# Moving three products of the accumulating bank to later slots in a seven-product block matmul

## The chip, the cores and the metric

The kernel runs on one core of a Trainium2 chip. The metric is the device time in microseconds (us) of one execution on that core. Executions are sorted into fast and slow by their time and granted clock. "The trace" is the profile of one of them.

## The reference

The input is x, 8 batches of 3008 x 256. A discrete Fourier transform over both axes (real part) is followed by an MLP mixer: token mixing through 256 hidden units, then channel mixing through 1536 hidden units, with residual additions.

```python
def reference(x, w_tok1, w_tok2, w_ch1, w_ch2):          # cut to what matters
    x = np.fft.fft(np.fft.fft(x, axis=1), axis=2).real
    h = np.maximum(x.transpose(0, 2, 1) @ w_tok1, 0.0) @ w_tok2
    u = x + h.transpose(0, 2, 1)
    h2 = np.maximum(u @ w_ch1, 0.0) @ w_ch2               # 256 -> 1536 -> 256: the larger part
    return u + h2
```

## The kernel before

The channel part runs in 48 chunks of 512 (or 448) tokens, six per batch. A chunk has twelve *slots*. In slot `ct`, TensorE computes one block of the hidden layer (`mm1`: two matmuls of 512 columns into `pc`; a *bank* here is a buffer that matmuls write and add into), and ScalarE takes it to memory with a ReLU. The second matrix, `h @ w_ch2`, is applied to the **previous** chunk between these slots. In 41 of the chunks it is not done as eight block products but as seven (a Winograd-type scheme): the blocks are combined first, in four *sums* on VectorE, and each product is twelve matmuls of 128 columns.

```python
def sums(c1, box, k):                    # VectorE; about 0.95 us each
    a11, a12, a21, a22 = quads(c1)
    ...
    if k == 1:   tt(box[1][:], a21, a22, AT.add)          # profile: s<-c
    elif k == 2: tt(box[2][:], box[1][:], a11, AT.subtract)   # s<-s,c
    elif k == 3: tt(box[3][:], a11, a21, AT.subtract)     # s<-c
    else:        tt(box[4][:], a12, box[2][:], AT.subtract)   # s<-c,s

def mm2_seven(b, c, c1, uT, k, box):
    ...
    if k == 0:                           # pa<-wc,c: opens the accumulating bank pa
        product(box["a"], a11, wc2[:, 0:NH, 0:P], True)
    ...
    if k < 0:    tt(q[:, 0], pa, u[:, 0], AT.add)         # a bank read: q<-pa,uT
    elif k == 1:                         # pb<-wc,c: the other bank
        product(pb, a12, wc2[:, NH:NCT, 0:P], True)
        tt(lo(0), halves(pb), q[:, 0], AT.add)            # osb<-pb,q
    elif k == 2:                         # pa<-t2w,s
        product(box["a"], box[2], t2w, False)
        tt(q[:, 1], pa, u[:, 1], AT.add)                  # q<-pa,uT
    elif k == 3: product(box["b"], box[1], t1w, True)     # pb<-t1w,s
    elif k == 4:                         # pa<-t3w,s
        product(box["a"], box[3], t3w, False)
        tt(q[:, 2], pa, u[:, 3], AT.add)
        tt(hi(1), halves(box["b"]), q[:, 2], AT.add)
    elif k == 5:                         # pa<-t4w,c
        product(box["a"], a22, t4w, False)
        tt(lo(1), pa, u[:, 2], AT.add)                    # osb<-pa,uT
    elif k == 6: ...                     # pb<-b,s, the last reads, and the store
```

The texts below call a product by its `k`: the second product is k = 2, and so on; k = 0 is a chunk's first. Products 0, 2, 4 and 5 all add into one bank, `pa`. VectorE must read the partial sum between them: product 4 may not write the bank before the read after product 2 has ended, and so on.

Which slot a product and a sum get stands in two tables. The order of issue within a slot is: hidden layer, product with its bank reads, sum, *front pieces*. A front piece is a part of the Fourier transform or token mixing of the next batch, with additions of its own on VectorE (`yt`, `ut` in the profile).

```python
sum_at = {0: 1, 1: 2, 3: 4, 4: 3}                                       # slot: sum
places = {0: 0, 1: -1, 2: 1, 4: 2, 6: 3, 7: 4, 9: 5, 11: 6}             # slot: product
...
for ct in range(NCT):
    mm1(b, c, c1, ct, on_v)
    ...
        if ct in places: mm2_seven(*prev, places[ct], pbox)
        if ct in sum_at: sums(prev[2], pbox, sum_at[ct])
    ...                                        # take(nxt, 1): front pieces
    if ct == 5 and ...:                        # GpSimd folds the input of a later batch
        if joins:                              # but only once the third sum is there
            G.tensor_copy(out=hold[:], in_=pbox[3][:, 0, 0, 0:1])
        n = min(left, 6 if c == 5 or b < 2 else 5)
        take(fold2, n)
```

## Time and profile before

| | |
|---|---|
| time, median of the first 3 runs | 603.53 us (602.35 to 603.78) |
| span in the trace | 600.3 us |
| TensorE busy | 583.2 us, 97% |
| from the first product (k = 0 of the first such chunk) to the end | 532.81 us |

These are lines of the page of the kernel before: the span, the busy time of TensorE (PE), its busy tenths in 40 slices, and the granted clock in tenths.

```profile
span 600.3 us, 15332 instructions
...
PE 583.2 (97%) x6273; PEld 417.3 (70%) x6273; DVE 452.8 (75%) x924; ACT 387.3 (65%) x753; POOL 259.3 (43%) x396
...
PE   3899999999999999999999999999999999999997
...
PEclk9999999999999999999999999999999999999999
```

TensorE is at nine tenths or more in all slices but the first two and the last. The Trainium skill's page "Perfetto Trace Analysis" warns in its opening that matmul busy time is a poor measure because matmuls are pipelined; this case agrees: before the second products the page of the kernel before shows 0.5 us of idle time, where the spacing used here shows 1.43 us of stalls. What I used instead is the *spacing*: the start of a matmul minus the start of the one before it. Its common values are 56 ns for 128 columns, 189 ns for 448 and 216 ns for 512. Whatever a spacing has over the common value is a stall of TensorE, whether or not the busy row shows it. Stalls of 20 ns and more are summed in this document.

The costliest groups on the page (line, engine, operation, output and inputs | busy us, mean ns of one | idle us before them and what ended it):

```profile
L712 PEld LDWEIGHTS <-s 128*128 128x128 f16 x1968 | 122.8, 98 | 40.1 <-DVE s L90 5.7
...
L90 DVE TENSOR_TENSOR q<-pa,uT 128x256 f32<-128x256 f32 x123 | 52.3, 425 | 36.3 <-PE pa L712 35.8
...
L712 PE MATMUL pa<-t2w,s 128*128 128x128 f16 x492 | 34.2, 219 | 0.5 <-DVE s L90 0.4
L712 PE MATMUL pa<-t3w,s 128*128 128x128 f16 x492 | 34.2, 219 | 0.3 <-DVE s L90 0.2
```

Only 0.5 us of idle time is shown before the second product (0.4 of it put down to a sum), but the weight loads of the products that take sums show 5.7 us of waits on VectorE. The loads run ahead of the matmuls, so most of those 5.7 us are hidden; the spacing says how much is not.

Here is a chunk without front pieces, from the timeline of the kernel before (start us, length us, engine, line, operation, out<-in, count):

```profile
552.49 0.84 PE L712 MATMUL pa<-wc,c 128*128 128x128 f16 x12
...
552.80 0.95 DVE L90 TENSOR_TENSOR s<-c 128x1536 f16<-128x1536 f16 x1
...
553.66 0.42 DVE L90 TENSOR_TENSOR q<-pa,uT 128x256 f32<-128x256 f32 x1
...
554.00 0.95 DVE L90 TENSOR_TENSOR s<-s,c 128x1536 f16<-128x1536 f16 x1
...
555.57 0.83 PE L712 MATMUL pa<-t2w,s 128*128 128x128 f16 x12
...
556.44 0.42 DVE L90 TENSOR_TENSOR q<-pa,uT 128x256 f32<-128x256 f32 x1 [0.24 <-PE pa L712]
556.78 0.95 DVE L90 TENSOR_TENSOR s<-c 128x1536 f16<-128x1536 f16 x1
...
557.10 0.83 PE L712 MATMUL pb<-t1w,s 128*128 128x128 f16 x12
...
558.20 0.83 PE L712 MATMUL pa<-t3w,s 128*128 128x128 f16 x12
```

Read it as a chain: first sum 552.80, bank read 553.66, second sum 554.00 (it ends 554.95), second product 555.57: a margin of 0.62 us. The third sum comes at 556.78, only after the bank read that follows the second product (556.44), and ends 0.47 us before the fourth product at 558.20. With no front work there is no stall.

With front work there is. Two stalls of the kernel before, from its timeline; the bracket is the idle time before an instruction and what ended it:

```profile
228.68 0.41 DVE L90 TENSOR_TENSOR q<-pa,uT 128x256 f32<-128x256 f32 x1
...
229.01 0.94 DVE L90 TENSOR_TENSOR s<-s,c 128x1536 f16<-128x1536 f16 x1
...
230.00 0.67 PEld L712 LDWEIGHTS <-s 128*128 128x128 f16 x12 [0.53 <-DVE s L90]
230.01 0.84 PE L712 MATMUL pa<-t2w,s 128*128 128x128 f16 x12
```

```profile
88.61 0.41 DVE L90 TENSOR_TENSOR q<-pa,uT 128x256 f32<-128x256 f32 x1
...
88.94 0.95 DVE L90 TENSOR_TENSOR s<-c 128x1536 f16<-128x1536 f16 x1
...
89.94 0.67 PEld L712 LDWEIGHTS <-s 128*128 128x128 f16 x12 [0.62 <-DVE s L90]
89.94 0.84 PE L712 MATMUL pa<-t3w,s 128*128 128x128 f16 x12
```

In the first, front additions put the bank read and the second sum late; the sum ends at 229.95 and the second product starts 0.06 us later, 0.20 us after TensorE could have. In the second, the third sum, behind the bank read, ends at 89.89 and the fourth product starts 0.06 us later, 0.30 us late. In the 41 chunks the trace of before has 6 stalls before second products (1.43 us) and 3 before fourth products (0.67 us). All nine end 57 or 58 ns after the end of that product's sum.

### The profile page before, as it was taken

How to read it: one execution, taken by the hardware profiler on the slowest of the kernel's cores; microseconds unless marked ns; L12 is line 12 of the kernel's file. 1: busy time of each engine (PE TensorE's matmuls, PEld its weight loads, DVE VectorE, ACT ScalarE, POOL GpSimd, SP SyncE). 2: the span in 40 equal slices, each digit the busy share in tenths (PEclk: the TensorE clock that was granted, in tenths of full speed). 3: DMA queues.
4: the chain of work that ended last, by engine and by line, in shares of the span. 5: the costliest groups of instructions: out<-in, count | busy, mean ns of one | idle time of the engine just before them, and what ended most of it. 6: DMA issues, size and time to landing. Idle time of an engine off the chain costs nothing.

```text
span 600.3 us, 15332 instructions
## 1 busy us (share of the span) xinstructions
PE 583.2 (97%) x6273; PEld 417.3 (70%) x6273; DVE 452.8 (75%) x924; ACT 387.3 (65%) x753; POOL 259.3 (43%) x396
## 2 busy tenths in 40 slices
PE   3899999999999999999999999999999999999997
PEld 3756676677767776667767777667767777666775
DVE  8779879686898668765898678856689757866663
ACT  8854665477647866577656866568665776546662
POOL 8650555937565554527348354565555100000000
PEclk9999999999999999999999999999999999999999
DMA  8993912275138914393335942278123422233533
GB/s 160 209 178 71 177 40 55 65 141 121 37 72 127 143 37 68 79 180 54 72 60 119 129 87 54 67 145 115 37 55 84 93 55 55 64 74 76 94 72 88
DMA packets 83414, 55.69 MB, mean 93 GB/s; under 512 B 53778, under 2 KB 80082, under 8 KB 82578
## 3 DMA queue, kind: packets, MB, share of 16 engines
q1 hardware_dynamic: 76816, 36.82, 32.2%
q0 software_dynamic: 6208, 17.63, 16.3%
q8 instruction: 49, 0.80, 0.6%
q10 hardware_dynamic: 320, 0.26, 0.2%
q14 instruction: 21, 0.17, 0.1%
HBM read 35.26 MB, written 24.64 MB: 100 GB/s over the span
## 4 chain that ended last, share of the span: by engine, by line
PE 81%; DVE 1%; issue 0%; ACT 0%; DVEq 0%
PE pc L662 35%; PE pa L712 17%; PE pb L712 13%; PE pu L566 5%; PE po L775 4%; PE pt L595 3%; PE pz L471 1%; PE py L538 1%; DVE s L90 1%; PE pw L508 1%; PE pw L512 1%; DVE osb L90 0%; DVE q L90 0%; DVE ut L90 0%; ACT c L97 0%
## 5 line engine op out<-in xcount | busy, mean ns | idle before, releaser
L97 ACT ACTIVATE c<-pc 128x512 f16<-128x512 f32 (+1 forms) x553 | 312.7, 591 | 159.9 <-PE pc L662 138.8
L662 PE MATMUL pc<-ut,wc 128*128 128x512 f16 (+1 forms) x1152 | 312.4, 374 | 0.4 <-DMA wc<-in_moe_w_ch_dram 0.3
L712 PEld LDWEIGHTS <-s 128*128 128x128 f16 x1968 | 122.8, 98 | 40.1 <-DVE s L90 5.7
L662 PEld LDWEIGHTS <-wc 128*128 128x128 f16 x1152 | 98.0, 98 | 55.7 <-issue 3.0
L712 PEld LDWEIGHTS <-c 128*128 128x128 f16 x1476 | 93.1, 97 | 27.8
L90 DVE TENSOR_TENSOR s<-c 128x1536 f16<-128x1536 f16 x82 | 82.0, 1000 | 4.7 <-ACT c L97 4.7
L90 DVE TENSOR_TENSOR q<-pa,uT 128x256 f32<-128x256 f32 x123 | 52.3, 425 | 36.3 <-PE pa L712 35.8
L908 POOL COPY hold<-s 128x1 f16<-128x1 f16 x29 | 5.4, 187 | 171.5 <-DVE s L90 171.5
L90 DVE TENSOR_TENSOR osb<-pb,q 128x256 f32<-128x256 f32 x123 | 51.9, 422 | 31.1 <-PE pb L712 28.4
L90 DVE TENSOR_TENSOR ut<-pu,yt 128x512 f16<-128x512 f32 (+1 forms) x96 | 63.0, 670 | 1.6 <-PE pu L566 1.5
L90 POOL TENSOR_TENSOR eo<-sab 96x512 f16<-96x512 f16 x48 | 53.9, 1139 | 1.6
L566 PE MATMUL pu<-w2r,uu 128*128 128x512 f16 (+1 forms) x168 | 50.0, 379 | 0.0
L90 POOL TENSOR_TENSOR sab<-fa,fb 96x256 f16<-96x256 f16 (+1 forms) x72 | 46.7, 673 | 0.0
L90 DVE TENSOR_TENSOR s<-s,c 128x1536 f16<-128x1536 f16 x41 | 41.1, 1003 | 0.0
L90 DVE TENSOR_TENSOR s<-c,s 128x1536 f16<-128x1536 f16 x41 | 39.5, 964 | 0.0
L97 ACT ACTIVATE w<-pw 128x257 f16<-128x257 f32 x90 | 34.6, 384 | 6.4 <-PE pw L512 3.6
L90 DVE TENSOR_TENSOR osb<-pa,uT 128x256 f32<-128x256 f32 x41 | 17.4, 424 | 24.8 <-PE pa L712 24.7
L775 PE MATMUL po<-wc,c 128*128 128x256 f16 x288 | 35.4, 273 | 0.0
L712 PE MATMUL pa<-t2w,s 128*128 128x128 f16 x492 | 34.2, 219 | 0.5 <-DVE s L90 0.4
L712 PE MATMUL pa<-t3w,s 128*128 128x128 f16 x492 | 34.2, 219 | 0.3 <-DVE s L90 0.2
L712 PE MATMUL pb<-wc,c 128*128 128x128 f16 x492 | 34.4, 219 | 0.0
L712 PE MATMUL pa<-wc,c 128*128 128x128 f16 x492 | 34.4, 219 | 0.0
(187 smaller groups left out, 747.8 us busy)
## 6 DMA issues: line engine op xcount, KB each, us to landing
out_dram<-osb SPq DMA_DIRECT2D x83, 256.0 KB
xp<-in_x_dram POOLq DMA_DIRECT2D x14, 408.0 KB, 6.6
out_dram<-osb SPq DMA_DIRECT2D x11, 192.0 KB
uT<-ut SPq DMA_TRANSPOSE x96
w2n<-in_moe_w_tok_dram POOLq DMA_DIRECT2D x2, 752.0 KB, 9.3
w1p<-in_moe_w_tok_dram POOLq DMA_DIRECT2D x2, 384.0 KB, 8.0
wc<-in_moe_w_ch_dram POOLq DMA_DIRECT2D x1, 768.0 KB, 14.7
xp<-in_x_dram POOLq DMA_DIRECT2D x2, 272.0 KB, 6.0
```

Source lines behind the costliest of these rows:

```text
L90: eng.tensor_tensor(out=out_, in0=a, in1=b, op=op)
L97: nc.scalar.activation(out=out_, in_=in_, func=func, scale=scale, **kw)
L471: nc.tensor.matmul(out_, lhsT=rows[:, half * P:half * P + P], rhs=tab, start=True, stop=True)
L508: nc.tensor.matmul(pw[:, 0:256].rearrange("p (h d) -> p h d", h=2)[:, :, 0:65], lhsT=zg[:, 0, g], rhs=td[:, 0:130].rearrange("p (h d) -> p ...
L512: nc.tensor.matmul(pw[:, 64:322].rearrange("p (h d) -> p h d", h=2)[:, :, 0:64], lhsT=zg[:, 1, g], rhs=td[:, 130:258].rearrange("p (h d) - ...
L538: nc.tensor.matmul(py[:, P * k:P * k + P], lhsT=w[:, 4 * c + k, o:o + P], rhs=tab[:, 4 * c + k, :], start=True, stop=True)
L566: nc.tensor.matmul(pu[:, 0:64 * nk], lhsT=uu[:, th, h, :], rhs=w2[:, th, :, 8 * c:8 * c + nk], start=(th == 0), stop=(th == 1))
L595: nc.tensor.matmul(pt[:, o:o + n], lhsT=hw[:, g, c], rhs=w[:, g, w0:w0 + n], start=(g == 0), stop=(g == NG - 1))
L662: nc.tensor.matmul(pc[:, 0:n], lhsT=wc1[:, h, ct * P:(ct + 1) * P], rhs=ut[:, c, h, 0:n], start=(h == 0), stop=(h == 1))
L712: nc.tensor.matmul(dst[:, P * a:P * a + P], lhsT=left[:, k, a, :], rhs=right[:, k, :], start=(first and k + a == 0), stop=(k == NH - 1), s ...
L775: nc.tensor.matmul(po[:, o:o + D], lhsT=c1[:, ct, ks * P:ks * P + P], rhs=wc2[:, ct, 0:D], start=(ct == 0), stop=(ct == NCT - 1))
L908: G.tensor_copy(out=hold[:], in_=pbox[3][:, 0, 0, 0:1])
```

## The change

The intent is to give the second product more time for its sum, and to shift the later products of the same bank along.

```diff
-    places = {0: 0, 1: -1, 2: 1, 4: 2, 6: 3, 7: 4, 9: 5, 11: 6}
+    places = {0: 0, 1: -1, 2: 1, 5: 2, 6: 3, 8: 4, 10: 5, 11: 6}
```

Number, shapes and operands of all instructions that the engines run stay.

## The prediction

> What bounds the kernel. The page: TensorE 583.2 us busy of a 600.3 us span (97%) at full clock. I took the start-to-start spacing of consecutive matmuls from the instruction timeline. The common spacing is 56 ns for 128 columns, 189 ns for 448 and 216 ns for 512. The Trainium skill, "TensorE: Matmul & The Clock Gate", section "Wait — 56ns, not 53.3ns?", gives 55.6 ns for 128 and 215.7 ns for 512 on a warm array, so the trace agrees: TensorE streams at its rate, the weight loads are hidden, and the time is the sum of matmul columns plus stalls. The spacing in excess of these values, counting stalls of 20 ns and more, adds up to only 12.1 us, 8.2 of it before 67 us, in the set-up and the first batch.
>
> What the change touches. In 41 chunks the seven products are placed among the twelve hidden-layer slots. Their number, shapes and operands stay. The change can only alter stalls. There I find these stalls of TensorE just before a product:
> - second product (accumulating bank, needs the second sum from VectorE): 6 stalls of 105 to 564 ns, 1.43 us together;
> - fourth product (needs the third sum): 3 stalls of 60 to 316 ns, 0.67 us together;
> - every other product: 0 (at most 1 ns each).
> So at most 2.1 us of 600 us, 0.35%, can be removed.
>
> Mechanism. The second sum follows the first on VectorE (about 0.95 to 1.2 us each, with a bank read between), and in a front-free chunk it ends 0.6 us before the second product starts. Slot 5 instead of 4 adds one hidden-layer slot, 0.43 us plus any front piece, to that margin. In order of issue the third sum was behind the read of the bank after the second product; now that read comes after it, so the third sum no longer waits for TensorE, and the fourth product comes a slot later. Front-free margin of the fourth product: 0.47 us before, over 1 us after. I expect 5 to 9 of the 9 stalls to go: 1.4 to 2.1 us.
>
> What may come back. The distance from second to fourth and from fourth to fifth product is unchanged, so the tight bank reuse (the read of the bank after the fourth product ends only 0.13 to 0.7 us before the fifth starts) stays. The fifth product comes one slot nearer to the next chunk's first, which reuses that bank: margin 1.3 us before in front-free chunks, about 0.9 us after. Slots 3 and 4 now both lack a product, so evacuations on ScalarE and front additions on VectorE bunch there; the three banks of each kind cover that. I allow 0.1 to 0.3 us for new stalls.
>
> Prediction: 603.5 - 2.0 + 0.2 = 601.7 us, range 600.5 to 603.5. Chances: faster by over 2% 0.01, within 2% 0.98, slower by over 2% 0.01.
>
> What would show it. Right: the summed spacing excess before the second and fourth products falls from 2.1 us to under 0.5 us; in the waits, the VectorE line that makes the sums nearly vanishes as a releaser of TensorE and its weight loads (5.7 us on weight loads before); TensorE's busy time otherwise the same; the third sum starts before the second product. Wrong: new stalls before the fifth product or the next chunk's first one, or before hidden-layer matmuls in slots 5 and 6 waiting for ScalarE, or the run-to-run spread of 1.4 us hiding it.

## The result, and the profile after

The changed kernel took 601.61 us (median of 6 runs, 601.25 to 602.58), the kernel before 602.98 us (median of 6, the three first ones among them). Ratios in this document are the mean time of one kernel's fast runs over that of the other's of the same rounds, so they are not quite the ratio of the medians: here 0.9979, with a 95% interval of 0.9967 to 0.9992. That is a real gain of about 1.3 us.

The page of the changed kernel, the lines that answer to those above:

```profile
span 599.8 us, 15331 instructions
...
PE 582.5 (97%) x6273; PEld 417.8 (70%) x6273; DVE 449.5 (75%) x924; ACT 390.2 (65%) x753; POOL 255.1 (43%) x396
...
L712 PEld LDWEIGHTS <-s 128*128 128x128 f16 x1968 | 123.5, 98 | 37.5 <-DVE s L90 0.6
...
L90 DVE TENSOR_TENSOR q<-pa,uT 128x256 f32<-128x256 f32 x123 | 52.5, 427 | 47.6 <-PE pa L712 47.5
...
L712 PE MATMUL pa<-t2w,s 128*128 128x128 f16 x492 | 34.2, 219 | 0.1
```

The wait of the weight loads for sums fell from 5.7 to 0.6 us. The idle time of VectorE before its bank reads rose from 36.3 to 47.6 us; that is no loss, it is VectorE now waiting for TensorE where TensorE waited for VectorE.

The same two places in the timeline of the changed kernel:

```profile
228.68 0.41 DVE L90 TENSOR_TENSOR q<-pa,uT 128x256 f32<-128x256 f32 x1
...
229.01 0.95 DVE L90 TENSOR_TENSOR s<-s,c 128x1536 f16<-128x1536 f16 x1
...
230.04 0.87 PEld L712 LDWEIGHTS <-s 128*128 128x128 f16 x12
...
230.26 0.83 PE L712 MATMUL pa<-t2w,s 128*128 128x128 f16 x12
```

```profile
88.97 0.95 DVE L90 TENSOR_TENSOR s<-c 128x1536 f16<-128x1536 f16 x1
...
89.84 0.42 DVE L90 TENSOR_TENSOR q<-pa,uT 128x256 f32<-128x256 f32 x1
...
90.67 0.50 PE L712 MATMUL pa<-t3w,s 128*128 128x128 f16 x6
```

In the first, the second sum ends where it did (229.96), but the second product starts at 230.26, without a wait. In the second, the third sum (88.97) is ahead of the bank read (89.84) and ends 0.75 us before the fourth product (90.67).

Over all 41 chunks, from the two traces:

| | before | changed |
|---|---|---|
| median margin, end of second sum to second product | 0.58 us | 1.10 us |
| median margin, end of third sum to fourth product | 0.63 us | 1.67 us |
| stalls before second and fourth products | 1.43 + 0.67 us | 0.26 + 0.05 us |
| other stalls after the first product | 1.75 us | 2.50 us |
| first product to the end | 532.81 us | 531.67 us |

So 1.79 us of stalls were taken away and 0.75 us came back, 1.04 us net; the other 0.1 us of the 1.14 us by which that stretch is shorter is in differences of under 20 ns. The largest that came back, 0.48 us by the spacing, is in the timeline of the changed kernel here:

```profile
98.91 0.94 DVE L90 TENSOR_TENSOR s<-s,c 128x1536 f16<-128x1536 f16 x1
...
99.65 0.54 PE L662 MATMUL pc<-ut,wc 128*128 128x448 f16 x2
99.78 0.68 DVE L90 TENSOR_TENSOR ut<-pu,yt 128x512 f16<-128x512 f32 x1
...
100.51 0.59 PE L566 MATMUL pu<-w2r,uu 128*128 128x512 f16 x2 [0.31 <-DVE ut L90]
```

A front matmul (`pu`) waits for a buffer that VectorE frees with an addition (`ut`, ends 100.46), which sits behind a sum. In the kernel before, the second product was in that place and covered the wait, and a fourth product stalled for 0.32 us a little later. Where VectorE itself is behind, the move shifts a stall rather than removing it. The second that came back, 0.17 us at 133 us, is a front matmul that waits for VectorE's copy of `z`.

The part ahead of the first product, which the change does not touch, took 67.5 us in one trace and 68.1 us in the other, and 67.5 to 68.6 us in all traces. That is why the spans (600.3 and 599.8 us) differ by less than the times do, and why traces are compared from the first product on. That stretch repeats well: a second trace of the changed kernel gave 531.70 against 531.67 us.

### The profile page after: what moved, and what is told of

Read it like the earlier page. It is cut to its first block, busy times and chain, and to the rows that moved or that the text cites. A ratio compares the mean times of both kernels' runs of the same rounds, so it can differ in the third digit from the quotient of the medians.

```text
span 599.8 us, 15331 instructions
## 1 busy us (share of the span) xinstructions
PE 582.5 (97%) x6273; PEld 417.8 (70%) x6273; DVE 449.5 (75%) x924; ACT 390.2 (65%) x753; POOL 255.1 (43%) x396
## 4 chain that ended last, share of the span: by engine, by line
PE 82%; DVE 1%; issue 0%; DVEq 0%
PE pc L662 36%; PE pa L712 17%; PE pb L712 13%; PE pu L566 6%; PE po L775 4%; PE pt L595 3%; PE pz L471 1%; PE py L538 1%; PE pw L512 1%; PE pw L508 1%; DVE s L90 1%; DVE osb L90 0%; DVE ut L90 0%; PE pz L496 0%; DVE q L90 0%
## 5 line engine op out<-in xcount | busy, mean ns | idle before, releaser
L662 PE MATMUL pc<-ut,wc 128*128 128x512 f16 (+1 forms) x1152 | 316.5, 374 | 1.2 <-DVE ut L90 1.2
L90 DVE TENSOR_TENSOR q<-pa,uT 128x256 f32<-128x256 f32 x123 | 52.5, 427 | 47.6 <-PE pa L712 47.5
L90 DVE TENSOR_TENSOR s<-c 128x1536 f16<-128x1536 f16 x82 | 80.7, 984 | 4.7 <-ACT c L97 4.7
L90 POOL TENSOR_TENSOR eo<-sab 96x512 f16<-96x512 f16 x48 | 52.7, 1114 | 1.6
L712 PE MATMUL pb<-t1w,s 128*128 128x128 f16 x492 | 34.2, 219 | 0.0
L712 PE MATMUL pa<-t4w,c 128*128 128x128 f16 x492 | 34.2, 219 | 0.0
```

The costliest lines, as they stand in the source:

```text
L90: eng.tensor_tensor(out=out_, in0=a, in1=b, op=op)
L662: nc.tensor.matmul(pc[:, 0:n], lhsT=wc1[:, h, ct * P:(ct + 1) * P], rhs=ut[:, c, h, 0:n], start=(h == 0), stop=(h == 1))
L712: nc.tensor.matmul(dst[:, P * a:P * a + P], lhsT=left[:, k, a, :], rhs=right[:, k, :], start=(first and k + a == 0), stop=(k == NH - 1), s ...
```

## The experiments

Twelve kernels were run, in three groups of four; each group shared one chip and its runs of the kernel before.

| run | time, us | before, us | ratio (95%) | first product to end, us | stalls before product 2 / 4, us |
|---|---|---|---|---|---|
| before (trace) | | | | 532.81 | 1.43 / 0.67 |
| e0_after | 602.30 | 603.44 | 0.9981 (0.9968 to 0.9994) | 531.70 | 0.27 / 0.04 |
| e1_second_only | 604.21 | 603.44 | 1.0017 (1.0004 to 1.0030) | 533.80 | 0 / 2.75 |
| e2_fourth_fifth | 603.11 | 603.44 | 0.9996 (0.9983 to 1.0009) | 532.70 | 1.58 / 0 |
| e3_no_sum_wait | 600.72 | 603.44 | 0.9963 (0.9950 to 0.9975) | 530.63 | 0 / 0 |
| e4_sums_first | 603.89 | 603.43 | 0.9999 (0.9977 to 1.0021) | 533.40 | 1.84 / 0.59 |
| e5_second_at_3 | 612.16 | 603.43 | 1.0147 (1.0124 to 1.0171) | 541.31 | 9.85 / 1.05 |
| e9_second_only_late_sum4 | 601.83 | 603.43 | 0.9971 (0.9953 to 0.9988) | 531.60 | 0.72 / 0.08 |
| e10_after_late_sum4 | 601.60 | 603.43 | 0.9972 (0.9955 to 0.9988) | 531.57 | 0.74 / 0 |
| e6_no_hold_before | 619.76 | 603.11 | 1.0279 (1.0260 to 1.0298) | 547.41 | 5.21 / 9.60 |
| e7_no_hold_after | 616.82 | 603.11 | 1.0219 (1.0201 to 1.0237) | 540.23 | 0.36 / 7.58 |
| e11_third_before_second | 606.40 | 603.11 | 1.0048 (1.0034 to 1.0063) | 536.08 | 0 / 0.11 |
| e12_late_sum4_fold5 | 605.41 | 603.11 | 1.0035 (1.0023 to 1.0047) | wrong result | |

### The changed kernel again

No edit.

> The changed kernel again, unedited. Theory A (margin: the gain is the removed waits of the second and fourth product for their sums): ratio near 0.998 again, 601 to 602 us; in the new trace the stalls before the second and fourth product are 0.2 to 0.5 us together (0.30 in the first trace of it, 2.10 before) and the time from the first product to the end is again near 531.7 us (532.8 before). Theory B (the 1.4 us are the chance of a lucky set-up, which differs by some 0.6 us between two traces): the ratio moves to 1.000, or the time from the first product on is as before.

The gain repeated in other rounds, and the trace from the first product on within 0.03 us. A lucky set-up (theory B) is out.

### The second product alone

```diff
-    places = {0: 0, 1: -1, 2: 1, 4: 2, 6: 3, 7: 4, 9: 5, 11: 6}
+    places = {0: 0, 1: -1, 2: 1, 5: 2, 6: 3, 7: 4, 9: 5, 11: 6}
```

> The kernel before with the second product alone in slot 5; the fourth stays in 7, the fifth in 9. Theory A: this alone takes nearly all the gain, since the third sum is then issued ahead of the bank read after the second product whatever the slot of the fourth: stalls before the second product 1.4 to about 0.3 us, before the fourth 0.67 to under 0.1; ratio 0.998, within 0.5 us of the changed kernel. Rival C (all three moves are needed): about a half to two thirds of the gain, with stalls left before the fourth product of 0.3 us or more.

This came out the other way. Stalls before second products did go, from 1.43 to 0. But those before fourth products rose to 2.75 us in nine chunks, and the kernel became 1.0 us slower than before. The timeline of one of them:

```profile
230.42 0.83 PE L712 MATMUL pa<-t2w,s 128*128 128x128 f16 x12
...
231.23 0.95 DVE L90 TENSOR_TENSOR s<-c 128x1536 f16<-128x1536 f16 x1
...
232.10 1.28 DVE L90 TENSOR_TENSOR yt<-py,sqy 128x512 f16<-128x512 f32 x2
...
233.30 0.41 DVE L90 TENSOR_TENSOR q<-pa,uT 128x256 f32<-128x256 f32 x1
...
233.77 0.83 PE L712 MATMUL pa<-t3w,s 128*128 128x128 f16 x12 [0.55 <-DVE q L90]
```

The third sum had ended at 232.18, 1.6 us before the fourth product. What the product waits for is the bank read at 233.30, which ends at 233.71; the product starts 0.06 us later. The read stands behind the third sum and two front additions in VectorE's queue. All nine stalls end 53 to 58 ns after such a read. The Trainium skill's page "PSUM — Partial Sum Buffer", section "Engine vs sequencer instructions", says that VectorE's queue is strictly first in, first out; this trace agrees, the read runs in its place in the order of issue although its bank had long been ready. So my theory was incomplete: moving the second product without the fourth cuts the time for *product, bank read, product* from three slots to two, and that is the tighter limit.

### The fourth and fifth alone

```diff
-    places = {0: 0, 1: -1, 2: 1, 4: 2, 6: 3, 7: 4, 9: 5, 11: 6}
+    places = {0: 0, 1: -1, 2: 1, 4: 2, 6: 3, 8: 4, 10: 5, 11: 6}
```

> The kernel before with the fourth product in slot 8 and the fifth in 10; the second stays in slot 4. Theory A: stalls before the fourth product go (0.67 to under 0.1 us), those before the second stay (1.4 us, plus or minus 0.3); the time falls by 0.3 to 0.7 us, ratio 0.999. Rival C: as much as half of the gain through other waits.

The stalls moved as expected (product 4 from 0.67 to 0, product 2 still 1.58), but only 0.11 us of the trace came of it, because other front stalls rose by 0.41 us and those before product 2 by 0.15. The time cannot be told from before's. The parts do not add: the second alone is 0.99 us worse in the trace, the fourth and fifth alone are 0.11 better, all three are 1.14 better.

### No wait for the sums at all

```diff
-            product(box["a"], box[2], t2w, False)
+            product(box["a"], box[1], t2w, False)
...
-            product(box["a"], box[3], t3w, False)
+            product(box["a"], box[1], t3w, False)
```

> The kernel before with its old slots, but the second and fourth product take the first sum as their stationary operand in place of the second and third (a wrong result on purpose; the sums are still computed). The first sum is long there, so both waits for sums are gone without moving anything. Theory A: stalls before both products 0 to 0.1 us; time as low as the changed kernel or up to 0.5 us below it, ratio 0.9965 to 0.998. Rival D (the gain comes from the new interleaving of products, hidden-layer matmuls and front pieces, not from the sums): no gain, ratio 1.000.

Its output is wrong, which doesn't matter for the time. With the old slots and the waits for the second and third sum gone, the trace is 2.18 us shorter from the first product on, against 2.10 us of stalls that the trace of before had there, and the ratio is 0.9963. No stall before any product is left. That confirms both the cause and the size of what there was to gain, and it shows that the waits can be taken away, and the time with them, without any new interleaving. The changed kernel gets about half of it (1.14 us).

### The second product a slot earlier

```diff
-    places = {0: 0, 1: -1, 2: 1, 4: 2, 6: 3, 7: 4, 9: 5, 11: 6}
+    places = {0: 0, 1: -1, 2: 1, 3: 2, 6: 3, 7: 4, 9: 5, 11: 6}
```

> The kernel before with the second product one slot earlier, in slot 3. Theory A (margin to the second sum): shifting each of the 41 second products to where the stream would have reached it a slot earlier, and letting it wait until 58 ns after its sum ended (the lag that all six stalls of before show), gives stalls before the second product of 8.9 us in 21 chunks, against 1.4 us in 6; so 6 to 9 us slower, ratio 1.010 to 1.015, with the stalls before the fourth product gone. Rival D (the slots matter by interleaving, not by the sum): within 2 us of before.

Measured: 9.85 us of stalls where 8.9 were worked out from the trace of before, and 8.7 us more time (medians). One slot of margin the other way costs about seven times what the change gains, since most chunks had little more than half a microsecond to spare. The waits of the weight loads for sums, 5.7 us over 12 waits before, are now these:

```profile
PEld L712 <- DVE s L90: 23.0, 42, 2.1
```

One part was wrong: stalls before fourth products did not go, they rose to 1.05 us.

### The sums ahead of the bank reads

```diff
-                    if ct in places:
-                        mm2_seven(*prev, places[ct], pbox)
                     if ct in sum_at:
                         sums(prev[2], pbox, sum_at[ct])
+                    if ct in places:
+                        mm2_seven(*prev, places[ct], pbox)
```

> The kernel before, old slots, but within a slot the sum is issued ahead of the product and its bank read: so the second sum before the read after the first product, the third sum before the read after the second. Theory A: the stalls before the fourth product go (0.67 to under 0.1 us), since the third sum was late only behind that read. Those before the second stay between 0.7 and 1.6 us, because the read now comes behind the second sum and the second product must wait for it instead (same bank): the queue of VectorE is what is late, not one instruction in it. Ratio 0.998 to 1.000. If the sum alone were late (rival), the second product's stalls fall by 0.4 us each, to under 0.3 us in all.

The stalls before the second product stayed, as theory A said, and were a little larger than its range (1.84 us). Every one now ends 53 to 58 ns after the bank read, which stands behind the sum. One more stall, 0.21 us before a fifth product, is new. My expectation for the fourth product was wrong for the same reason that I had given for the second: 0.59 us stay, now behind the read. The product needs both; changing which of the two comes last in the queue changes nothing. What is late is VectorE's queue.

### A shorter queue ahead of the bank read

On top of the kernel with the second product alone moved:

```diff
-    sum_at = {0: 1, 1: 2, 3: 4, 4: 3}
+    sum_at = {0: 1, 1: 2, 3: 3, 5: 4}
...
-                            G.tensor_copy(out=hold[:], in_=pbox[3][:, 0, 0, 0:1])
+                            G.tensor_copy(out=hold[:], in_=pbox[4][:, 0, 0, 0:1])
```

> The run with the second product alone moved lost 1.0 us: its stalls before the fourth product rose to 2.75 us in 9 chunks, each ending 53 to 58 ns after VectorE's read of the accumulating bank. Theory E (turnaround of the bank: second product, read, fourth product; two slots are too few because the read queues behind sums and front additions on VectorE): keep that placement, but issue the third sum in slot 3 and the fourth sum only after the read, in slot 5 (GpSimd's hold then waits for the fourth sum). The read comes up to 0.95 us earlier in VectorE's queue, so the stalls before the fourth product fall from 2.75 to under 0.6 us, and the time from the first product to the end from 533.8 to 531.2 to 532.0 us; ratio 0.997 to 0.999. Rival F (the fourth product waits for something else, or for the third sum): 2 us or more of stalls remain.

The fourth sum is needed only for the last product. Taking it out from in front of the bank read brought the stalls before the fourth product from 2.75 to 0.08 us, and a placement that had lost 1.0 us then gained as much as the change does (531.60 us), although two stalls before second products (0.72 us) were back. The edit also moves the third sum a slot earlier, but in the run with the second product alone that sum had ended 0.39 us or more before each of the nine stalled products, so it was not what they waited for. This is direct evidence for the bank turnaround, and for its dependence on what stands in the queue.

### The same on top of the change

The same edit on the changed kernel.

> The changed kernel with the same order of sums (third in slot 3, fourth in slot 5 behind the bank read). A try at a better version. Stalls before the fourth product 0.04 to 0; the stall of about 0.26 us before a second product, where the second sum took 1.48 us, stays; time from first product to end 531.2 to 531.7 us, ratio 0.997 to 0.998. Against it: GpSimd's fold starts a slot later and may run into the next chunk's sums, which would put 0.2 to 0.5 us of new stalls before second products.

It is correct, and its trace is 0.1 us shorter than the changed kernel's (531.57 us); by time the two cannot be told apart. What it gained, it lost elsewhere, in the way named as the risk: GpSimd starts its fold a slot later, runs into the next chunk's sums and slows them. In its timeline a first sum takes 1.50 us while GpSimd works, and the second product behind it stalls for 0.36 us:

```profile
225.29 1.31 POOL L90 TENSOR_TENSOR sab<-fa,fb 96x256 f16<-96x256 f16 x2
...
225.92 1.50 DVE L90 TENSOR_TENSOR s<-c 128x1536 f16<-128x1536 f16 x1
...
228.87 0.94 DVE L90 TENSOR_TENSOR s<-s,c 128x1536 f16<-128x1536 f16 x1
...
229.87 0.84 PE L712 MATMUL pa<-t2w,s 128*128 128x128 f16 x12 [0.19 <-DVE s L90]
```

In the changed kernel GpSimd is earlier and ends before that sum, which takes 0.95 us:

```profile
225.04 1.31 POOL L90 TENSOR_TENSOR sab<-fa,fb 96x256 f16<-96x256 f16 x2
...
226.61 0.95 DVE L90 TENSOR_TENSOR s<-c 128x1536 f16<-128x1536 f16 x1
```

### Without GpSimd's hold

On the kernel before and on the changed one:

```diff
-                        if joins:
-                            G.tensor_copy(out=hold[:], in_=pbox[3][:, 0, 0, 0:1])
```

> The kernel before without the one-element copy by which GpSimd waits for the third sum before each batch of fold pieces; GpSimd then runs its fold as soon as its data are there, also under VectorE's sums. In the traces so far sums of which more than 0.3 us lay under GpSimd work took 1.27 us in the mean and the others 0.95. Theory G (GpSimd's fold stretches the sums, and this uses up the margin of the second product): many more sums over 1.05 us than the 14 of before, stalls before the second product of 4 to 12 us, time up by 3 to 12 us. Rival (the hold only costs GpSimd its idle time): time within 1 us of before.

> The changed kernel without the same hold. Theory A with G: the sums are stretched as much, but the second product has a slot more to spare, so the loss is smaller: stalls before the second and fourth product at least 2 us below those of the kernel before without the hold, and the gap between the two placements grows from 1.3 us to 2 to 6 us. If the placement has nothing to do with the lateness of sums, the gap stays at 1.3 us.

Letting GpSimd run freely costs 2.8% with the old placement. In that trace the sums that lie mostly under GpSimd work take 1.26 us in the mean, the others 0.95; bank reads, which take one operand from the bank and one from memory, take 0.42 us either way (mean 0.428 and 0.422). The Trainium skill's page "SBUF — State Buffer", section "Who interferes with whom", says that a VectorE instruction with two memory inputs contends with a GpSimd instruction that reads memory, and one with at most one such input, outside certain faster modes, does not; the numbers agree. Stalls before the second product were 5.2 us, within the expected range; those before the fourth, of which I had said nothing, were 9.6 us, and the loss of 16.7 us is above the expected 12.

Not all of this loss is shown to come from stretched sums. In the two largest stalls of that trace (1.67 us at 137.8 us, 2.63 us at 143.4 us) VectorE's bank read had itself waited 2.53 and 2.19 us for a transpose by DMA (`uT`), a kind of wait that the traces of the kernel before and of the changed kernel do not have; and the matmuls after the second of them ran at a granted clock of 0.50, which cost about 1.7 us by the spacing. Together that is some 6 of the 14.6 us that the trace lost from the first product on. Why the transposes were late was not tested.

With the changed placement the ratio is 1.0219, so the gap between the placements was 0.6% (1.0279 less 1.0219), about 3.6 us, against 1.3 us with the hold. That is in the expected range, but it is the weaker evidence (the plain means of all runs of the two kernels are 4.2 us apart): this kernel's five runs spread from 609.9 to 617.4 us, with granted clocks from 0.993 to 0.999, and its trace is of the fastest. In it, second products hardly stall (0.36 us) and fourth products stall on bank reads (7.6 us).

### The third product ahead of the second

```diff
-    places = {0: 0, 1: -1, 2: 1, 4: 2, 6: 3, 7: 4, 9: 5, 11: 6}
+    places = {0: 0, 1: -1, 2: 1, 4: 3, 6: 2, 8: 4, 10: 5, 11: 6}
```

> The kernel before with the third product (the other bank, first sum) in slot 4 and the second in slot 6, the fourth in 8, the fifth in 10. Theory E (bank turnaround): no stall before the second product, but second and fourth now have only one bare slot and no product between them, about 0.86 us less the 0.67 us that drain, read and semaphore take where the read is not queued; so stalls before the fourth product that end 53 to 58 ns after the bank read, 2 to 8 us in all, and a time above the kernel before. If the sums alone mattered, it would be as good as the changed kernel, 0.998.

It is slower, as the bank theory said, but not where I said: the fourth product stalls for 0.11 us only. The third does, for 5.4 us in 18 chunks, on the *other* bank. It now follows product 1 in that bank by two slots, and the read between them stands behind the second sum:

```profile
195.87 0.95 DVE L90 TENSOR_TENSOR s<-s,c 128x1536 f16<-128x1536 f16 x1
...
196.73 0.42 DVE L90 TENSOR_TENSOR osb<-pb,q 128x256 f32<-128x256 f32 x1
...
197.20 0.83 PE L712 MATMUL pb<-t1w,s 128*128 128x128 f16 x12 [0.45 <-DVE osb L90]
```

So the rule holds for either bank, and I had checked it for one only. The second product, with its sum ready, does not stall at all, so its sum alone is not what decides a placement.

### A smaller batch of fold pieces

```diff
-                        n = min(left, 6 if c == 5 or b < 2 else 5)
+                        n = min(left, 5)
```

> The changed kernel with the later fourth sum, and GpSimd's fold in batches of at most 5 pieces in place of 6 in some chunks, so that it ends before the next chunk's sums. A try at the last 0.38 us stall, before a second product whose second sum took 1.48 us under GpSimd. Theory G: that sum takes 0.95 us, that stall goes, and the time from the first product to the end falls from 531.57 to 531.1 to 531.3 us; ratio 0.996 to 0.998, not to be told from the changed kernel's by time. Against it: the fold of a batch takes a chunk more, which moves the front of the next batch and may make stalls elsewhere.

The result was wrong (relative error 0.15), so its time says nothing. The likely reason, argued from the code and not tested, is that the start of the next batch's front is computed for six pieces a chunk, and so it was issued ahead of the end of the fold. Whether the 0.26 us stall left in the changed kernel can be removed by moving the fold stays open.

## Why the prediction was right, and where it was not

- **What bounds the kernel** was right. TensorE streams, and the change moves stalls only. The no-wait run put the ceiling at 2.18 us where the prediction had 2.1.
- **The margin of the second product** was right in mechanism and size: 0.62 to 1.05 us in front-free chunks, one slot of 0.43 us. Five of its six stalls are gone, the sixth fell from 0.56 to 0.26 us.
- **The third sum no longer waiting for the second product** was right, but the sign given for it was wrong. The third sum *starts before the second product* in only 6 of 41 chunks. It starts before that product *ends* in 31 (0 before the change), which is what counts, since earlier the bank read, and so the end of the product, had to come first. The margin of the fourth product in front-free chunks went from 0.47 to 1.57 us ("over 1 us").
- **"The distance from second to fourth ... is unchanged"** was right and carries more than I gave it. I counted the move of the fourth product as extra margin for the third sum. The experiments show that its real work is to keep the bank turnaround: without it the change loses 1.0 us.
- **"The fifth product comes one slot nearer to the next chunk's first"**: 0.9 us was predicted for what is left of the margin in front-free chunks, 0.91 us was measured, and no stall.
- **What comes back** was mis-sized and misplaced. The prediction allowed 0.1 to 0.3 us, before the fifth or the first product or at hidden-layer matmuls. 0.75 us came, before front matmuls that wait for VectorE. With 1.79 us taken away where 2.0 was said, the net in the trace is 1.14 us from the first product on, and in the times 1.2 to 1.4 us (1.1 in the repeat), not 1.8.
- **The figure of 601.7 us** met 601.61 us a little by luck: the gain was smaller than said, but the kernel before also came out at 602.98 us over six runs, not 603.53.

No version that is clearly better was found. Two with the later fourth sum are as good as the changed kernel, with ratios of 0.9971 and 0.9972. The no-wait run says that about 1.0 us more could be had from these two waits and what they displace.

## What to carry to other kernels

When the bottleneck engine streams, look for its stalls in the spacing of its instructions and add up only those that a change can reach; that gives the ceiling before anything is tried. A matmul that takes an operand from a busy engine and adds into a bank which that engine reads has two deadlines, the operand and the bank, and both stand in one queue: moving one product later without those that follow it in the same bank trades the first wait for the second. Ahead of such a read, put nothing into the queue that is not needed yet.

## What the Trainium skill lacked or had wrong

- "TensorE: Matmul & The Clock Gate", section "What's actually happening", has the clock fall to half after an idle window of about 3.4 us. Here, in the one such event of these traces, about 2.5 us of idle time was enough: in the kernel before without the hold TensorE stood idle from about 140.9 to 143.4 us, and the granted clock was 0.50 for the next 3.4 us. Windows of that run's trace (start:end and length in us, busy us and instructions of each engine, granted clock, DMA share, GB/s):

```profile
core 0: us, PE busy (x) PEld busy (x) DVE busy (x) ACT busy (x) POOL busy (x), PEclk, DMA share, GB/s
...
140.90:143.40 2.50, 0.03 (x1) 0.00 (x1) 1.81 (x2) 0.60 (x1) 2.50 (x4) 1.00 1.21 318
143.60:146.80 3.20, 3.20 (x21) 2.09 (x19) 0.85 (x2) 1.26 (x3) 3.12 (x5) 0.50 0.47 50
```

- "PSUM — Partial Sum Buffer" names the hazard of a bank being read while TensorE writes it, but I found no figure there for the turnaround. Here a matmul that waited for VectorE started 52 to 59 ns after the end of the read or sum, over all such stalls whose end could be matched to one instruction.
- "SBUF — State Buffer", section "Who interferes with whom", says that the one that comes second blocks fully. It gives no figure for additions of this size; here a 128 x 1536 sum of two 16-bit operands took 1.26 us in the mean under GpSimd and 0.95 us alone.
